# A planner that orders attention and a long convolution on one core: hand-written rules for the next task, against weighted sums with eight sets of weights

## The chip, the cores and the metric

The kernel runs on one core of a Trainium2 chip. The metric is the time of one execution in microseconds of device time. TensorE (PE) does the matmuls, VectorE (DVE) and ScalarE (ACT) empty its results from PSUM and do the elementwise work, GpSimd (POOL) issues the loads that change the type, and SyncE (SP) issues the other transfers.

## The reference

```python
# attention: batch 8, seq 3136, d_model 256, d_qk 64
scores = (1.0 / S) * np.matmul(z, z.transpose(0, 2, 1))
attn = np.maximum(scores, 0.0) ** 2
x = u * np.matmul(attn, v)
# then a gated long convolution over the sequence
proj = x @ w_proj                                  # 256 -> 768: x1, x2, x3
X2 = np.fft.rfft(x2, n=S, axis=1)
H = np.fft.rfft(filter_fft, n=S, axis=0)[None, :, :]
x2_conv = np.fft.irfft(X2 * H, n=S, axis=1)
y = x1 * x2_conv * x3
out = (y @ w_out).astype(np.float32)
```

The scores are symmetric in the two positions, and there is no softmax. The inputs are float32; the kernel computes with bfloat16 operands and float32 sums.

## The kernel before, in words

For each of the 8 batches the 3136 rows are cut into 7 chunks of columns (512, 512, 512, 512, 512, 256, 320), and for each chunk the score tiles of 128 rows are made in pairs. A score task (kind S) multiplies two 64-row operands at once in two halves of the array, or, cut further, in four quarters. ScalarE takes the relu of the pair (tile R_t, L1762), and VectorE (L1771) or ScalarE (L1769) squares it (A_t). A weighing task (kind W) multiplies the square by v and adds it up in one of two PSUM accumulators, ps_o. Some squares are also transposed by a DMA (M_t, M2e_t, M2o_t) and weighed again in a later chunk, because the scores are symmetric. At the end of a chunk VectorE multiplies the accumulators by u (xT_t, L1813), which frees them for the next chunk.

The rest of the network is made of other tasks of PE. Kind FA is a chunk's projections (wp) with the first step of its transform; their results go to gates (L1157) or through DRAM to the next step of the transform. Kind Q is the middle of the transform in quarters of the array, forward (S) and inverse (TZ), with a multiplication by the filter on VectorE (L1245) between. Kind FB ends the transform and applies w_out, and yT_t (L1331) is the gated product before that. Kind FZ holds such tasks of the last two batches that are kept back for the end. PSUM has three pairs of banks (ps_s) for all results but the weighing's; a score or a Q task takes a whole pair, the others one bank. Every matmul passes line 518, every copy out of PSUM line 551 (ScalarE) or 555 (VectorE).

No queue or loop fixes the order of this work. All tasks are first written down with what they depend on, what buffers they take and a cost in microseconds for each engine that can do them; then `Plan.go` plays the program through, always starting the task that can start first, and emits the instructions of each engine in that order. On the chip each engine goes through its own list and waits at semaphores. So the planner's choices are the order, and nothing is chosen at run time.

For PE, `pick_pe` looks at the first few tasks of each kind and goes through rules with fixed limits: stay with the scores while a pair of banks is free, go back to them when two or three pairs are free, put a Q task into a run of scores (the whole run is then cut into quarters, `plan.quarters`), do weighing or projections first by a `credit` that weighing earns (PACE) and other work spends. For the other engines, `pick` takes the task that can start first, in steps of 0.03 us, and among equals the one with the lower `prio`.

The diff touches the constants at the head of the file, these functions, and the two places that cut scores and short weighings into quarters:

Of the kernel before, what the change touches and what calls it, by code (L numbers as in the profile page):

```python
# [11 lines left out]
P = 128  # L12
# [6 lines left out]
N1 = 64  # L19
# [1 line left out]
NJ = 16  # L21
CHUNKS = (512, 512, 512, 512, 512, 256, 320)
INF = float("inf")
PACE = 0.45
HOLD = 3
DELAY = 4
GROUP = 1
BACKLOG, AMPLE, STAY = 1.5, 5.0, 0.1
LATE_PUT, LATE_LOAD, LATE_TURN, LATE_C, LATE_D2 = 3.0, 1.0, 1.5, 2.5, 1.0
SPEC_LAG = 1  # L30
LATE_F = 6.0
# [2 lines left out]
FINAL = (0, 2, 4, 6, 1, 3, 5)  # L34
ZP, ZL = 0, 0.0
MOST = 3
FULL = 3.0
QUAD, FIRST, LEAD = -INF, 1.0, 0
YIELD = 1.0
REACH = 2  # L40
SHARE = {0: 1, 2: 3}

# [117 lines left out]
class Task:  # L160


    def __init__(self, emit, cost, deps=(), takes=(), prio=0, lat=None, moves=0.0, late=0.0):
        self.emit, self.cost, self.takes, self.prio = emit, cost, list(takes), prio
        self.lat, self.moves, self.late = lat, moves, late
        self.deps = [d if isinstance(d, tuple) else (d, None) for d in deps]
        self.kids, self.frees = [], []
        self.left = len(self.deps)
        self.ready = 0.0
        self.end = None  # L170
        self.holders = 1
        for d, _ in self.deps:
            d.kids.append(self)
# [9 lines left out]
class Plan:  # L183


    def __init__(self):
        self.free = {e: 0.0 for e in ("PE", "ACT", "DVE", "SP", "POOL")}
        self.queues = {"S": [], "Q": [], "W": [], "FA": [], "FB": [], "FZ": []}
        self.pend = {e: [] for e in ("ACT", "DVE", "SP", "POOL")}
        self.credit = 0.0  # L190
        self.mode = None
        self.quarters = False
        self.quad_run = self.score_run = 0
        self.soon = False
        self.n = 0
        self.spare = []
        self.pairs = None
        self.bus = 0.0
# [70 lines left out]
    def queued(self, t):  # L269
        some = {id(x): x for e in ("ACT", "DVE") for x in self.pend[e] if x.ready <= t + 0.3}  # L270
        return sum(max(0.0, self.free[e] - t) for e in ("ACT", "DVE")) + sum(min(x.cost.values()) for x in some.values())

    def pick_pe(self):
        t = self.free["PE"]
        got = {}
        for k, window in (("S", 1), ("Q", 4), ("W", 1), ("FA", 6), ("FB", 6), ("FZ", 6)):
            best = None
            for task in self.queues[k][:window]:
# [3 lines left out]
            if best:  # L282
                got[k] = best
        if not got:
            return None
        more = self.queues["S"]
        quad = got.pop("Q", None)
        if self.mode == "S" and self.quarters and quad and quad[0] <= t + STAY:
            if not more or self.quad_run < 1 and self.score_run >= LEAD:
                return (*quad, "Q")  # L290
        if more and not more[0].left:
            left = self.backlog()
            if self.mode == "S":
                if "S" in got and got["S"][0] <= t + STAY:
                    return (*got["S"], "S")
                got.pop("S", None)
                if self.quarters and quad and quad[0] <= t + STAY and self.quad_run < 1:
                    return (*quad, "Q")
            else:
                want = 3 if left > AMPLE else 2  # L300
                free = self.pairs.when(min(want, len(more)) - 1)
                first = quad and quad[0] <= t + 0.3 and left > FIRST and self.credit > QUAD
                if "S" in got and free > t + 0.04:
                    rest = {k: v for k, v in got.items() if k != "S" and (k == "W" or left > BACKLOG)}
                    if rest and min(v[0] for v in rest.values()) < free:
                        got = rest
                    elif free < INF:
                        if first and not LEAD:
                            return max(quad[0], free), quad[1], "Q"
                        self.soon = bool(first)  # L310
                        return max(got["S"][0], free), got["S"][1], "S"
                elif "S" in got:
                    if first and not LEAD:
                        return (*quad, "Q")
                    self.soon = bool(first)
        elif quad:
            got["Q"] = quad
        if not got and quad:
            return (*quad, "Q")
        if not got:  # L320
            return None
        near = t + 0.04
        order = ["S", "Q"]
        order += ["FA", "FB", "W", "FZ"] if self.credit > 0 and self.queued(t) < FULL else ["W", "FA", "FB", "FZ"]
        for k in order:
            if k in got and got[k][0] <= near:
                return (*got[k], k)
        k = min(got, key=lambda k: (got[k][0], order.index(k)))
        return (*got[k], k)

    def pick(self, e):
        t = self.free[e]
        best = None
        for task in self.pend[e]:
            s = max(t, self.ready_at(task))
            if s == INF:
                continue
            first = next(iter(task.cost))
            if e != first:
                behind = sum(  # L340
                    x.cost[first] for x in self.pend[first]
                    if x is not task and x.prio <= task.prio and next(iter(x.cost)) == first and x.ready <= s + 0.3
                )
                end = s + task.cost[e]
                held = max((end - max(x.ready, s) for x in self.pend[e] if len(x.cost) == 1 and x.ready < end), default=0.0)
                if end + YIELD * held >= max(self.free[first], task.ready) + behind + task.cost[first]:
                    continue
            key = (round(s / 0.03), task.prio, task.no)
            if best is None or key < best[0]:
                best = (key, s, task)  # L350
        return best and (best[1], best[2], e)

    def go(self):
        while True:
            got = []
            x = self.pick_pe()
            if x:
                got.append((x[0], 0, x[1], "PE", x[2]))
            for i, e in enumerate(self.pend):
                x = self.pick(e)  # L360
                if x:
                    got.append((x[0], i + 1, x[1], e, None))
            if not got:
                break
            start, _, task, e, k = min(got, key=lambda g: g[:2])
            if k:
                self.queues[k].remove(task)
                half = k in ("S", "Q")
                if half != (self.mode == "S") and self.mode:
                    start += 0.096  # L370
                    self.quarters, self.quad_run, self.score_run = half and self.soon, 0, 0
                self.score_run += k == "S"
                if k == "Q":
                    self.quad_run += 1
                    if self.score_run and not self.quarters:
                        start += 0.092
                    self.quarters = True
                self.mode = "S" if half else k
                if k == "W":
                    self.credit = min(self.credit + PACE, 2.0)  # L380
                elif k != "S":
                    self.credit = max(self.credit - task.cost["PE"], -2.0)
            self.run(task, e, start)
        left = sum(len(q) for q in self.queues.values()) + sum(len(q) for q in self.pend.values())
        assert not left, f"{left} tasks left over"
# [3 lines left out]
def kernel(  # L389
# [12 lines left out]
    B, S, D = u.shape  # L402
# [23 lines left out]
    plan = Plan()  # L426
# [1141 lines left out]
    def score_mm(un, where):  # L1568
# [6 lines left out]
        for i in order[: len(pair)] if len(pair) != 3 else (0, 2, 1):  # L1575
            (t, at), h = pair[i], ds((i if len(pair) <= 2 else i // 2) * dqk, dqk)
            o = blocks(ps, len(pair), cw)[:, i]
            for m in range(0, P, N1 if plan.quarters else P):
                n = N1 if plan.quarters else P
                matmul(o[ds(m, n)], zt[h, ds(t * P + m, n)], zt[h, ds(C0[at], cw)], start=True, stop=True)  # L1580
        live[un] = ps

# [131 lines left out]
    def weigh_short(b, c):  # L1714
        cw = CHUNKS[c]
        un, i = short[b, c][1:]
        for dh in range(2):
            h = ds(dh * N1, N1)
            for m in range(0, P, N1 if plan.quarters else P):
                n = N1 if plan.quarters else P  # L1720
# [5 lines left out]
    for gi, g in enumerate(groups):  # L1726
# [23 lines left out]
        for i, un in enumerate(g):  # L1750
# [13 lines left out]
            def sq(e, un=un, rows=rows, n=n, cw=cw, box=box, a_p=a_p):  # L1764
# [142 lines left out]
```

## Time and profile before

| | |
|---|---|
| time, median of 3 runs | 1000.24 us (999.77 to 1001.09) |
| span of the profiled execution | 996.6 us |
| PE busy | 956.2 us, 6831 matmuls |
| ScalarE busy | 878.6 us |
| VectorE busy | 826.4 us |
| first matmul and last matmul | 4.9 us after the start, 8.0 us before the end |
| DMA moved | 170.33 MB, mean 171 GB/s |
| granted TensorE clock | 0.996 |

The span is the time from the first to the last instruction of one profiled execution, and the time of a run is some microseconds more. PE's busy time is what its matmuls cover, overlaps counted once; the ends of matmuls are modelled. The page gives such sums, groups of instructions by line, and the chain that ended last; the trace behind it gives the same for any stretch of time, what an engine waited for, and a timeline in which equal instructions in a row are merged (start, length, engine, line, count).

### The profile page before, as it was taken

How to read it: one execution, taken by the hardware profiler on the slowest of the kernel's cores; microseconds unless marked ns; L12 is line 12 of the kernel's file. 1: busy time of each engine (PE TensorE's matmuls, PEld its weight loads, DVE VectorE, ACT ScalarE, POOL GpSimd, SP SyncE). 2: the span in 40 equal slices, each digit the busy share in tenths (PEclk: the TensorE clock that was granted, in tenths of full speed). 3: DMA queues.
4: the chain of work that ended last, by engine and by line, in shares of the span. 5: the costliest groups of instructions: out<-in, count | busy, mean ns of one | idle time of the engine just before them, and what ended most of it. 6: DMA issues, size and time to landing. Idle time of an engine off the chain costs nothing. (4 is left out here: it accounts for less than half of the span.)

```text
span 996.6 us, 19588 instructions
## 1 busy us (share of the span) xinstructions
PE 956.2 (96%) x6831; PEld 470.0 (47%) x6831; DVE 826.4 (83%) x1447; ACT 878.6 (88%) x1205; POOL 187.2 (19%) x403
## 2 busy tenths in 40 slices
PE   6999999999999999999999999999999999999975
PEld 2343544346444554435544464444644356444643
DVE  8975689987788788888789878887888969889785
ACT  5987799989899898989998989999889989999774
POOL 5142311122011210213021131113201122000000
PEclk9999999999999999999999999999999999999999
DMA  9899868788998798888999888997899879865676
GB/s 157 145 176 184 142 127 176 148 158 176 196 174 149 157 177 194 177 174 140 193 204 184 150 174 167 201 187 146 160 208 182 159 137 197 210 142 126 161 217 205
DMA packets 332376, 170.33 MB, mean 171 GB/s; under 512 B 242442, under 2 KB 307786, under 8 KB 332276
## 3 DMA queue, kind: packets, MB, share of 16 engines
q1 hardware_dynamic: 304548, 138.10, 62.8%
q0 software_dynamic: 27728, 30.97, 22.3%
q8 instruction: 54, 0.88, 0.4%
q14 instruction: 46, 0.38, 0.1%
HBM read 90.26 MB, written 53.35 MB: 144 GB/s over the span
## 5 line engine op out<-in xcount | busy, mean ns | idle before, releaser
L1762 ACT ACTIVATE R_t<-ps_s 128x1024 f32<-128x1024 f32 (+4 forms) x512 | 470.3, 956 | 40.5 <-PE ps_s L518 26.2
L518 PE MATMUL ps_o_t<-A_t,v_t 128*128 128x512 bf16 (+6 forms) x2074 | 462.0, 354 | 6.3 <-DVE A_t L1771 6.0
L1771 DVE TENSOR_TENSOR A_t<-R_t 128x1024 bf16<-128x1024 f32 (+1 forms) x291 | 330.9, 1150 | 67.2 <-ACT R_t L1762 62.4
L518 PEld LDWEIGHTS <-v_t 128*128 128x128 bf16 (+1 forms) x2878 | 250.2, 98 | 271.6 <-issue 83.0
L1769 ACT ACTIVATE A_t<-R_t 128x1024 bf16<-128x1024 f32 (+4 forms) x205 | 196.4, 964 | 5.3 <-DMA M_t<-A_t 2.2
L518 PE MATMUL ps_s<-zT_t 64*64 64x512 bf16 (+4 forms) x1485 | 158.4, 359 | 2.8 <-ACT x_t L551 1.0
L601 POOL COPY tick<-xT_t 1x1 bf16<-1x1 bf16 x54 | 12.4, 230 | 709.8 <-DVE xT_t L1813 693.8
L518 PE MATMUL ps_s<-xT_t,wp 128*128 128x512 bf16 (+2 forms) x430 | 103.5, 352 | 3.8 <-DVE xT_t L1813 1.4
L551 ACT ACTIVATE x_t<-ps_s 128x512 bf16<-128x512 f32 (+2 forms) x137 | 74.1, 568 | 21.2 <-PE ps_s L518 12.7
L1813 DVE SCALAR_TENSOR_TENSOR xT_t<-ps_o_t,uT_t 128x256 bf16<-128x256 f32 (+2 forms) x224 | 76.0, 381 | 19.3 <-PE ps_o_t L518 11.5
L1245 DVE TENSOR_TENSOR xh<-xh,H 128x1024 bf16<-128x1024 bf16 x120 | 82.3, 686 | 6.6 <-ACT xh L551 2.7
L518 PEld LDWEIGHTS <-zT_t 64*64 64x64 bf16 (+1 forms) x1518 | 56.2, 101 | 66.0 <-issue 49.6
L518 PE MATMUL ps_o_t<-M_t,v_t 128*128 128x512 bf16 (+2 forms) x352 | 82.2, 353 | 0.0
L1157 DVE TENSOR_TENSOR gate_t<-ps_s,x_t 128x256 bf16<-128x256 f32 (+2 forms) x216 | 71.8, 382 | 10.5 <-PE ps_s L518 7.6
L518 PEld LDWEIGHTS <-wp 128*128 128x128 bf16 x448 | 42.7, 98 | 48.9 <-issue 11.7
L1331 DVE TENSOR_TENSOR yT_t<-ps_s,gate_t 128x512 bf16<-128x512 f32 (+2 forms) x97 | 57.8, 620 | 8.1 <-PE ps_s L518 6.4
L592 POOL DMA_DIRECT2D un_t<-in_u_dram x112 | 59.9, 555 | 7.8 <-issue 4.6
L611 POOL DMA_DIRECT2D v_t<-in_v_dram x112 | 59.5, 556 | 4.9 <-issue 2.8
L518 PE MATMUL ps_s<-wp,xT_t 128*128 128x256 bf16 x398 | 56.1, 273 | 0.3 <-DVE xT_t L1813 0.2
L551 ACT ACTIVATE gs_t<-ps_s 128x512 bf16<-128x512 f32 (+1 forms) x89 | 50.6, 605 | 5.9 <-PE ps_s L518 5.5
L518 PE MATMUL ps_s<-wo,yT_t 128*128 128x256 bf16 (+1 forms) x362 | 53.8, 273 | 1.7 <-DVE yT_t L1331 1.7
L555 DVE CAST x_t<-ps_s 128x512 bf16<-128x512 f32 (+2 forms) x73 | 46.0, 641 | 10.5 <-PE ps_s L518 8.3
(147 smaller groups left out, 824.1 us busy)
## 6 DMA issues: line engine op xcount, KB each, us to landing
out_dram<-ost_t SPq DMA_DIRECT2D x66, 256.0 KB
spec<-s_t SPq DMA_DIRECT2D x96, 128.0 KB
spec_in_t<-spec SPq DMA_DIRECT2D x60, 192.0 KB
spec<-gs_t SPq DMA_DIRECT2D x60, 192.0 KB
v_t<-in_v_dram POOLq DMA_DIRECT2D x80, 128.0 KB, 4.5
un_t<-in_u_dram POOLq DMA_DIRECT2D x80, 128.0 KB, 5.0
conv_in_t<-spec SPq DMA_DIRECT2D x33, 256.0 KB
out_dram<-ost_t SPq DMA_DIRECT2D x19, 128.0 KB
```

Of the source, the lines that this page charges most:

```text
L518: wrote(nc.tensor.matmul(o, *args, **kw), o)
L551: got = nc.scalar.activation(out_, in_, AF.Copy)
L555: got = nc.vector.tensor_copy(out_, in_)
L592: nc.gpsimd.dma_start(out=t[ds(j * N1, N1), lo - t0 : hi - t0, :], in_=x[:, n2 : n2 + hi - lo, :])
L611: nc.gpsimd.dma_start(out=t[ds(j * N1, N1), ds(v_at(a), (b - a) * D)], in_=r[:, n2 + a - lo : n2 + b - lo, :].rearrange("p t d -> p (t d)"),)
L1157: got = nc.vector.tensor_tensor(g[:, ::-1] if h == 0 else g, p, x, ALU.mult)
L1245: nc.vector.tensor_tensor(x[:, 1 - i], x[:, 0], h, ALU.mult)
L1331: got = nc.vector.tensor_tensor(yb["y"][:, dh, 0:w], p, gates[b, c, dh][:, 0:w], ALU.mult)
L1762: has_read(nc.scalar.activation(blocks(box["R"], n, cw)[:rows], p, AF.Relu), p)
L1769: nc.scalar.activation(a, r, AF.Square)
L1771: nc.vector.tensor_tensor(a, r, r, ALU.mult)
L1813: nc.vector.scalar_tensor_tensor(x, f, inv_s2, ut, ALU.mult, ALU.mult)
```

## The change

The rules in `pick_pe` go. For the first few tasks of each kind the kind's candidate is found as before, and then one number is worked out for it: how long PE would stand until it can start, plus a price for changing the array's arrangement times a weight (`turn`), plus nine weights of its kind times nine numbers of the state. These are 1, the evictions queued (`queued`), the weighing that is ready (`backlog`), the credit, the free banks, the length of the present run, the free pairs, and how long the second and the third pair still need. The lowest number is taken. Scores in a run that began in halves stay in halves; they are cut into quarters only if the run has had a Q task (`mode` 2).

The weights come from one of eight sets, "a" to "h". A string of 187 letters, MIX, names the set for each stretch of twelve PE tasks; the plan has 2244 of them. The pace at which weighing earns credit comes from the set too.

For the other engines, `pick` adds a bias by rank to the start (-0.03 to 0.09 us) in place of the steps of 0.03 us and the strict `prio`; `give` takes the place of the constant YIELD. Ranks come from `prio` by (2, 3, 4, 5, 0)[prio], so tasks with prio 4 have the same rank as those with prio -1.

```diff
-PACE = 0.45
-BACKLOG, AMPLE, STAY = 1.5, 5.0, 0.1
-FULL = 3.0
-QUAD, FIRST, LEAD = -INF, 1.0, 0
-YIELD = 1.0
+SWITCH, QUARTER = 0.096, 0.092
+KINDS = {"S": 1, "Q": 4, "W": 1, "FA": 6, "FB": 6, "FZ": 6}
+WEIGHTS = {
+    "a": Weights(
+        1.395, 0.797, 2.224, (-0.03, 0.0, 0.0, 0.03, 0.06, 0.09),
+        S=(-0.016, -0.197, 0.206, -0.053, -0.117, -0.017, -0.366, 0.385, 0.73),
+        Q=(-1.226, 0.38, -0.129, 1.049, -0.235, 0.074, -0.055, 0.599, -0.351),
+        W=(0.422, -0.009, -0.077, -0.062, 0.08, 0.007, 0.665, -0.522, 0.017),
+        FA=(-0.26, 0.123, 0.021, -0.232, 0.123, 0.099, 0.3, -0.453, -0.001),
+        FB=(0.819, -0.04, 0.086, -0.343, -0.295, 0.133, 0.206, -0.228, 0.033),
+        FZ=(2.581, -0.139, 0.697, 0.542, -0.157, 0.139, -0.368, 0.005, 0.316),
+    ),
...
+STRETCH = 12
+MIX = (
+    "chbeegbghbaageecebgfecfgbadeeedffbcgebdcgbececaahhfbceddhcdegbdhdhegdefcehbcagec"
...
+        self.rank = (2, 3, 4, 5, 0)[prio]
...
+    def weights(self):
+        return WEIGHTS[MIX[min(self.done // STRETCH, len(MIX) - 1)]]
+
+    def state(self, t):
+        at = self.pairs.banks.at
+        some, left = self.queued(t), self.backlog()
+        empty = sum(x <= t for pair in at for x in pair)
+        whole = sorted(max(pair) for pair in at)
+        second, third = ((min(max(x - t, 0.0), 2.0) if not self.mode else 0.0) for x in whole[1:])
+        return 1.0, some, left, self.credit, empty, self.length, sum(x <= t for x in whole), second, third
...
+            s, task = best
+            mode = max(self.mode or 0, 1) if kind == "S" else 2 * (kind == "Q")
+            turn = 0.0
+            if self.mode is not None and mode != self.mode:
+                turn = QUARTER if self.mode == 1 and mode == 2 else SWITCH
+            worth = s - t + turn * weights.turn
+            for w, x in zip(weights.kinds[kind], state):
+                worth += w * x
+            if got is None or worth < got[0]:
+                got = worth, s + turn, task, kind, mode
+        return got and got[1:]
...
-                if end + YIELD * held >= max(self.free[first], task.ready) + behind + task.cost[first]:
+                if end + give * held >= max(self.free[first], task.ready) + behind + task.cost[first]:
...
-            key = (round(s / 0.03), task.prio, task.no)
+            key = (s + ranks[task.rank], task.no)
...
-            for m in range(0, P, N1 if plan.quarters else P):
-                n = N1 if plan.quarters else P
+            for m in range(0, P, N1 if plan.mode == 2 else P):
+                n = N1 if plan.mode == 2 else P
...
+            r_.rank = 1
```

The last line gives the relus rank 1. No task, cost, buffer or dependence is changed.

More of the change, by code (lines that the diff above doesn't have):

```diff
@@ L40 @@
+STRETCH = 12
+MIX = (
+    "chbeegbghbaageecebgfecfgbadeeedffbcgebdcgbececaahhfbceddhcdegbdhdhegdefcehbcagec"
+    "abbbdgfdgbdhchhdchcaedhfhhaeacbaadeebfaaabfccdgdffdfaacccfebchccdabdfbdbeeccafae"
+    "fhchhgabfghcchhgdfgdeggaaaa"
+)
 REACH = 2
@@ L191, in __init__ @@
         self.mode = None
-        self.quarters = False
-        self.quad_run = self.score_run = 0
-        self.soon = False
+        self.length = self.done = 0
         self.n = 0
@@ L271, in queued @@
         return sum(max(0.0, self.free[e] - t) for e in ("ACT", "DVE")) + sum(min(x.cost.values()) for x in some.values())
+    def weights(self):
[7 more added lines that the diff above has]
+        return 1.0, some, left, self.credit, empty, self.length, sum(x <= t for x in whole), second, third
     def pick_pe(self):
-        t = self.free["PE"]
-        got = {}
-        for k, window in (("S", 1), ("Q", 4), ("W", 1), ("FA", 6), ("FB", 6), ("FZ", 6)):
+        t, weights = self.free["PE"], self.weights()
+        state = self.state(t)
+        got = None
+        for kind, window in KINDS.items():
             best = None
-            for task in self.queues[k][:window]:
+            for task in self.queues[kind][:window]:
                 s = max(t, self.ready_at(task))
@@ L281, in pick_pe @@
                     best = (s, task)
[L282 to L329, printed above, removed]
+            if best is None:
+                continue
@@ L331, in pick @@
+        return got and got[1:]
     def pick(self, e):
         t = self.free[e]
+        ranks, give = self.weights().ranks, self.weights().give
         best = None
@@ L357, in go @@
             if x:
-                got.append((x[0], 0, x[1], "PE", x[2]))
+                got.append((x[0], 0, x[1], "PE", *x[2:]))
             for i, e in enumerate(self.pend):
@@ L361, in go @@
                 if x:
-                    got.append((x[0], i + 1, x[1], e, None))
+                    got.append((x[0], i + 1, x[1], e, None, None))
             if not got:
                 break
-            start, _, task, e, k = min(got, key=lambda g: g[:2])
+            start, _, task, e, k, mode = min(got, key=lambda g: g[:2])
             if k:
                 self.queues[k].remove(task)
[L368 to L378, printed above, removed]
+                if mode != self.mode and (self.mode, mode) != (1, 2):
+                    self.length = 0
+                self.mode = mode
+                self.length += 1
                 if k == "W":
-                    self.credit = min(self.credit + PACE, 2.0)
+                    self.credit = min(self.credit + self.weights().pace, 2.0)
                 elif k != "S":
                     self.credit = max(self.credit - task.cost["PE"], -2.0)
+                self.done += 1
             self.run(task, e, start)
@@ L1718, in weigh_short @@
             h = ds(dh * N1, N1)
-            for m in range(0, P, N1 if plan.quarters else P):
-                n = N1 if plan.quarters else P
+            for m in range(0, P, N1 if plan.mode == 2 else P):
+                n = N1 if plan.mode == 2 else P
                 matmul(
```

67 lines of the change are left out of this document (added).

## The prediction

> **What bounds the kernel now.** I read the page's header and busy line first, then the busy time by stretch, then what TensorE (PE) waited for in the middle, and last the timeline around changes of its arrangement and near the end.
>
> ```profile
> span 996.6 us, 19588 instructions
> PE 956.2 (96%) x6831; PEld 470.0 (47%) x6831; DVE 826.4 (83%) x1447; ACT 878.6 (88%) x1205; POOL 187.2 (19%) x403
> 0.00:50.00 50.00, 39.38 (x206) 15.75 (x207) 44.47 (x98) 36.98 (x45) 15.99 (x40) 1.00 0.90 150
> 50.00:930.00 880.00, 865.99 (x6129) 421.36 (x6128) 737.21 (x1257) 801.60 (x1085) 171.26 (x363) 1.00 0.86 169
> 930.00:997.00 67.00, 50.80 (x500) 32.89 (x498) 44.70 (x93) 40.04 (x76) 0.00 (x0) 0.94 0.72 206
> ```
>
> The last three rows are stretches: us, then busy PE, PEld, DVE, ACT, POOL, clock, DMA share, GB/s. PE is idle 10.6 us at the start, 14.0 us in 880 us of middle, 16.2 us at the end, 40.8 in all; ScalarE and VectorE have 78 and 143 us to spare in the middle. So PE's instruction stream is the bound, and the change rewrites only its order. The profiled execution's span is 996.6 us against a median of 1000.24 us; I take the 3.6 us around the span as fixed.
>
> What ended PE's idle time in the middle (us, times, longest):
>
> ```profile
> PE ps_o_t L518 <- DVE A_t L1771: 4.0, 8, 0.8
> PE ps_o_t L518 <- DVE xT_t L1813: 3.7, 7, 1.0
> PE ps_s L518 <- ACT R_t L1762: 1.9, 3, 1.3
> PE ps_s L518 <- DVE xT_t L1813: 1.7, 5, 0.7
> PE ps_s L518 <- ACT x_t L551: 1.1, 3, 0.4
> PE ps_s L518 <- ACT s_t L551: 0.8, 2, 0.7
> PE ps_s L518 <- DVE x_t L555: 0.3, 2, 0.2
> ```
>
> Three kinds: weighing waits for a square (4.0); a chunk's turn, where VectorE must empty the accumulators, as xT_t, before the next chunk's weighing (3.7) or its own projections (1.7) can start; and a score bank that is not yet emptied (R_t, x_t, s_t, x_t: 4.1).
>
> **The change, part by part.** It alters no task. In the two instruction orders as built, DMA, POOL and full-array matmul counts are equal; 271 matmuls go (6831 to 6560), since fewer scores are cut into quarters: four 64x64 quarters and two 64x128 halves stream for the same time, so this alone is worth nothing. Rival one, that the change does not do what it says, is out: hardly a line of PE's order stays in place.
>
> *Changes of arrangement.*
>
> ```profile
> 410.28 1.04 PE L518 MATMUL ps_o_t<-A_t,v_t 128*128 128x512 bf16 x4
> 411.25 0.41 PE L518 MATMUL ps_s<-xh,TZ 64*64 64x512 bf16 x4
> 411.49 0.60 PE L518 MATMUL ps_s<-zT_t 64*64 64x512 bf16 x8
> 412.02 1.04 PE L518 MATMUL ps_o_t<-A_t,v_t 128*128 128x512 bf16 x4
> 932.85 0.43 PE L518 MATMUL ps_o_t<-A_t,v_t 128*128 128x320 bf16 x2
> 933.67 0.71 PE L518 MATMUL ps_o_t<-A_t,v_t 128*128 128x320 bf16 x4
> 934.31 0.31 PE L518 MATMUL ps_s<-zT_t 64*128 64x320 bf16 x2
> 934.45 0.30 PE L518 MATMUL ps_o_t<-A_t,v_t 64*128 64x320 bf16 x2
> 934.59 0.30 PE L518 MATMUL ps_s<-zT_t 64*128 64x320 bf16 x2
> 934.82 0.39 PE L518 MATMUL ps_s<-x_t,T 128*128 128x512 bf16 x1
> ```
>
> A 512-column matmul takes (1.04-0.39)/3 = 0.217 us from start to start, a 320-column one (0.71-0.43)/2 = 0.14. Four from 410.28 are through at 411.15 and the quarters start at 411.25; their three groups of 0.21 would be through by 411.89 and the full array starts at 412.02: a visit to quarters costs 0.23. Four from 933.67 are through at 934.23, the halves start at 934.31; the last pair is through at 934.73, the full array starts at 934.82: with rounding, 0.2 a visit. The order as built has 160 visits to halves instead of 127 and 97 to quarters instead of 123: 33 x 0.2 - 26 x 0.23 = **+0.6 us**, all on PE's path. The Trainium skill, "TensorEngine Tiling (Array Packing)", Key Properties, says that changing the tiling mode drains the array, which speaks against the 7 visits more. The trace agrees, in the 0.1 us at each edge; by that rule alone the time would be 1000.8.
>
> *Waits in the middle.* For each task of PE I counted the PE work (columns at the paces above) that the order puts between the matmul that feeds it and the task itself.
>
> Weighing after its square: the chain is relu, square, hand-overs:
>
> ```profile
> L1762 ACT ACTIVATE R_t<-ps_s 128x1024 f32<-128x1024 f32 (+4 forms) x512 | 470.3, 956 | 40.5 <-PE ps_s L518 26.2
> L1771 DVE TENSOR_TENSOR A_t<-R_t 128x1024 bf16<-128x1024 f32 (+1 forms) x291 | 330.9, 1150 | 67.2 <-ACT R_t L1762 62.4
> ```
>
> That is 2.1 us with nothing queued, and up to one more relu and square, 4.2, where the engines are busy. Tasks with under 4.5 us of cover: 57 before, 16 after. In that proportion 4.0 becomes 1.1: **-2.9** (bounds -4.0 and 0).
>
> Projections after the chunk's xT_t: under 2 us of cover 80 before, 1 after; the 1.7 goes: **-1.7**. Next chunk's weighing after it: turns with under 1.2 us of cover 10 before, 6 after; 3.7 becomes 2.2: **-1.5** (bounds -3.7 and +1).
>
> Banks: this gets worse. Reuses of a score bank with under 1.2 us of PE work since its last matmul: 56 before, 101 after (under 1.4 us: 162 and 254). What fills the room won above is projections, and their banks are turned round at once. In proportion 4.1 becomes 7.4, +3.3; but few of the 56 waited at all (10 waits on banks in the whole list), which would make it +0.9 for 45 more at 0.02. I take **+2.0**, between them.
>
> ScalarE and VectorE: about 20 squares go to VectorE and 18 copies to ScalarE. At 1.15 us the squares are 23 us more on VectorE before the copies are taken off, of its 143 spare: nothing. If that cover were gone, it would be on the path in full.
>
> Middle: -2.9 - 1.7 - 1.5 + 2.0 = **-4.1**.
>
> *The end.* The last batch's spectrum is a chain through DRAM, and what work of PE is left beside it counts.
>
> ```profile
> 942.35 0.98 PE L518 MATMUL ps_o_t<-A_t,v_t 128*128 128x320 bf16 x6
> 945.54 0.49 PE L518 MATMUL ps_s<-x_t,T 128*128 128x512 bf16 x2
> 948.91 2.92 SPq L991 DMA_DIRECT2D spec_in_t<-spec  x6
> 954.69 0.63 PE L518 MATMUL ps_s<-spec_in_t,S 49*64 49x256 bf16 x9
> 957.00:963.00 6.00, 4.18 (x68) 2.46 (x68) 6.00 (x11) 6.00 (x13) 0.00 (x0) 1.00 0.85 284
> 963.00:970.00 7.00, 5.09 (x85) 2.81 (x85) 5.92 (x11) 5.49 (x12) 0.00 (x0) 0.84 0.78 220
> 970.00:978.00 8.00, 6.94 (x36) 3.44 (x35) 4.90 (x15) 4.49 (x9) 0.00 (x0) 0.92 0.53 155
> 956.25 5.49 SPq L1390 DMA_DIRECT2D out_dram<-v_t  x6
> 971.01 1.75 SPq L1290 DMA_DIRECT2D spec<-uT_t  x3
> 973.95 4.33 SPq L1003 DMA_DIRECT2D A_t<-spec  x7
> ```
>
> The last weighing is the row at 942.35. The new order puts 10 projections of 512 columns and one transform more behind it: 11 x 0.217 = 2.4 us less stands ahead of it, and behind it PE idles 16 us anyway. The order also brings the first forward transform nearer to the last weighing (49 matmuls between, not 84) and spreads the withheld output work over 957 to 978, where PE is idle. In 957 to 970 VectorE is busy 11.92 of 13 us, so that stretch will not shrink; I count the 2.4 once: **-2.4**. Bounds: -6.5, half of what PE idles here before its last matmul on top; and +2.6 for the queue: four of the six out_dram<-v_t stores now stand in SP's queue between the spec<-uT_t puts and the last loads A_t<-spec, at 5.49/6 = 0.92 us each 3.7, of which the gap from 972.76 to 973.95 hides 1.2.
>
> The clock dips to 0.84 and 0.92 here. The Trainium skill, "TensorE: Matmul & The Clock Gate", Part 1, has the clock fall after an idle window of about 3.4 us and return after a busy one; the trace agrees in so far as the dip lies where PE idles most. By that rule a denser stretch would win at most 0.16 x 7 + 0.08 x 8 = 1.8 us more. I leave it out, since the evictions bind there.
>
> *The start.* The first 11 us of work are almost the same sequence; PE waits for data: 0 (-1 to +1).
>
> Sum: +0.6 - 4.1 - 2.4 = -5.9 on 1000.24: **994.3 us**.
>
> **Rivals.** *More is won.* If no bank waits more, the turns' 3.7 goes too and the end yields its 6.5: 0.6 - 4.0 - 1.7 - 3.7 - 6.5 = -15.3, **985**. For it: the cover grew at every data dependence. Against: bank cover shrank.
>
> *The end gives it back.* The stores ahead of the last loads delay the final chain by 2.6 and the 2.4 is lost: 0.6 - 4.1 + 2.6 = -0.9, **999.3**, no change. For it: SP's new order. Against: 164 matmuls, not 132, now follow the last inverse transform and can run beside those loads.
>
> *Slower: the banks.* A copy that finds a relu of 0.956 us on ScalarE holds its bank that much longer. The 92 more reuses under 1.4 us would, at 0.15 us each, cost 13.8 where I put 2.0: -5.9 + 11.8 = +5.9, **1006**. It turns the sign past 0.086 us each. For it: ScalarE is busy 91% of the middle. Against: reuses this close hardly waited before.
>
> **Chances.** Forecast 0.52, more 0.20, given back 0.14, banks 0.14. About 0.2% (2 us) is what a measurement of this kernel can tell from no change. Faster: 0.50 of the forecast's 0.52 and the 0.20, 0.70; same: 0.14 and the rest of the forecast's, 0.16; slower 0.14. The range leaves out most of the bank case and the far end of the big gain: 986.5 to 1001.5; the forecast's own is 990 to 998.
>
> **What would show it.** Right: middle idle of PE near 10 us with A_t and xT_t rows small and R_t and x_t rows larger; the last weighing about 6 us earlier and its distance to the end the same. Wrong: bank rows over 10 us in the middle; or PE's last matmul over 8 us before the end, with A_t<-spec issued over 4 us after the spec<-uT_t puts.

## The result, and the profile after

The changed kernel took 985.5 us, the median of four executions (981.70, 983.38, 987.62, 987.84), against 1000.38 us for the kernel before (four, 999.77 to 1001.09): a ratio of 0.9852, 95% interval 0.9825 to 0.9878. In a later round six more executions gave 988.48 us (984.62 to 991.65); over all ten the median is 987.0. Beside these six the kernel before took 1000.52 us. So the gain is 12 to 15 us where 5.9 had been forecast, and the kernel after spreads over 10 us (981.70 to 991.65) where the one before spreads over 4 (998.27 to 1002.35 in all rounds). The median of all ten lies at the edge of the forecast's range of 986.5 to 1001.5; the size of the gain was forecast at under half either way.

The profile of the 981.70 us execution of the kernel after, header and busy line:

```profile
span 979.9 us, 18879 instructions
PE 940.6 (96%) x6450; PEld 468.4 (48%) x6560; DVE 827.4 (84%) x1449; ACT 872.4 (89%) x1203; POOL 186.2 (19%) x403
```

Its busy time by stretch (us, then busy PE, PEld, DVE, ACT, POOL, clock, DMA share, GB/s), cut where its middle ends:

```profile
0.00:50.00 50.00, 39.48 (x205) 15.78 (x209) 43.01 (x96) 37.71 (x47) 16.53 (x42) 1.00 0.87 148
50.00:923.00 873.00, 861.79 (x5850) 427.44 (x5951) 746.55 (x1275) 801.44 (x1094) 169.67 (x362) 1.00 0.91 173
923.00:980.00 57.00, 39.38 (x399) 25.15 (x400) 37.89 (x79) 33.29 (x65) 0.00 (x0) 0.90 0.70 204
```

What ended TensorE's idle time in 50 to 923 us (us, times, longest):

```profile
PE ps_o_t L575 <- issue: 3.5, 22, 0.2
PE ps_s L575 <- DVE s_t L612: 2.0, 1, 2.0
PE ps_s L575 <- DMA spec_in_t<-spec: 0.9, 1, 0.9
PE ps_s L575 <- issue: 0.2, 1, 0.2
PE ps_o_t L575 <- DVE x_t L612: 0.2, 1, 0.2
```

The rows of `issue` are places where a matmul's record is missing from the trace (6450 of 6560 are there); no engine waits in them. Without them 3.1 us are left, of 13.5 before: the rows of A_t, of xT_t and of R_t have gone, and that of the copies x_t is 0.2. What stands there instead are two single waits, 2.0 and 0.9 us, that hang on transfers to and from DRAM (below). The window's idle time, 873.00 - 861.79 = 11.2 us, says less than it seems: 7.5 of it stand at 98 places of missing records, and 3.7 are idle, of 14.0 before.

Yet PE is 96% busy in both kernels, and while the middle's list fell by 10.4 us, the last weighing came 20 us earlier (943.02 to 923.02, counted at its last matmul). The reason is how a wait is drawn. Two rows of PE's timeline in the kernel before:

```profile
771.69 0.59 PE L518 MATMUL ps_o_t<-A_t,v_t 128*128 128x512 bf16 x2
773.10 1.24 PE L518 MATMUL ps_o_t<-A_t,v_t 128*128 128x512 bf16 x5 [0.81 <-DVE A_t L1771]
```

Two matmuls of 0.217 us from start to start begin at 771.69; the next could start at 772.12 and starts at 773.10, 0.97 us late after rounding. The view calls 0.81 of that idle, since it draws each matmul about 0.16 us past the start of the next. So every wait is listed 0.16 us short, and those under 0.16 us not at all. The Trainium skill, "Perfetto Trace Analysis", opening note, calls matmul busy time a bad metric for how close a kernel is to the roofline, because matmuls are pipelined; this case agrees, with 96% on both sides of a change of 15 us.

I therefore measured each kernel from start to start: the time between two matmuls less the pace of the first one's shape (0.217 us for 512 columns, shared by the matmuls that run side by side in halves or quarters) and less 0.1 us for each edge of an arrangement. The sum of the paces and edges is "work"; the rest is waiting. "Middle" runs from 35 us of work to the last weighing, "end" from there to the last matmul:

| us | before | after |
|---|---|---|
| first matmul starts | 4.9 | 5.3 |
| work | 927.7 | 928.5 |
| waits up to 35 us of work | 9.6 | 9.0 |
| waits in the middle | 30.1 | 12.6 |
| of these ahead of weighings | 18.6 | 4.9 |
| waits at the end | 16.2 | 15.6 |
| last matmul's start to the end of the span | 8.3 | 9.0 |

The middle's -17.4 is the whole gain between these two profiles; the other rows sum to +0.7, and the span falls by 16.7. Single waits over 0.4 us in the middle: some 21 with 15 us before, and after only the two named above, with 3.1 us. The sizes hang on the pace: most pairs of 512 columns start 0.2155 us apart, and with that in place of 0.217 the middle has 35.5 us before and 17.8 after. The difference stays. How the waits after fall to weighings and to the rest is uncertain by some 2 us, since 110 records are missing there.

### The profile page after: what moved, and what is told of

Its sections match the earlier page's. It is cut to its first block, busy times and chain, and to the rows that moved or that the text cites. A ratio compares the mean times of both kernels' runs of the same rounds, so it can differ in the third digit from the quotient of the medians.

```text
span 979.9 us, 18879 instructions
## 1 busy us (share of the span) xinstructions
PE 940.6 (96%) x6450; PEld 468.4 (48%) x6560; DVE 827.4 (84%) x1449; ACT 872.4 (89%) x1203; POOL 186.2 (19%) x403
## 4 chain that ended last, share of the span: by engine, by line
PE 88%; DMA 4%; DVE 3%; ACT 2%; issue 1%; SPq 1%; ACTq 0%; DVEq 0%
PE ps_o_t L575 52%; PE ps_s L575 36%; DVE A_t L1828 1%; DMA spec_in_t<-spec 1%; DMA ost_t<-in_z_dram 1%; ACT R_t L1819 1%; DMA spec<-gs_t 1%; SPq L700 1%; DMA conv_in_t<-spec 1%; DMA spec<-s_t 0%; DMA A_t<-spec 0%; DVE yT_t L1388 0%; ACT xh L608 0%; ACT gs_t L608 0%; SPq L1447 0%
## 5 line engine op out<-in xcount | busy, mean ns | idle before, releaser
L1819 ACT ACTIVATE R_t<-ps_s 128x1024 f32<-128x1024 f32 (+4 forms) x512 | 473.7, 957 | 53.6 <-PE ps_s L575 39.3
L575 PE MATMUL ps_o_t<-A_t,v_t 128*128 128x512 bf16 (+3 forms) x1998 | 465.0, 354 | 8.0 <-issue 3.5
L1828 DVE TENSOR_TENSOR A_t<-R_t 128x1024 bf16<-128x1024 f32 (+3 forms) x312 | 346.1, 1128 | 77.6 <-ACT R_t L1819 76.9
L575 PEld LDWEIGHTS <-v_t 128*128 128x128 bf16 (+2 forms) x2846 | 249.8, 98 | 271.1 <-issue 88.4
L1826 ACT ACTIVATE A_t<-R_t 128x1024 bf16<-128x1024 f32 (+4 forms) x184 | 181.2, 990 | 2.1
L575 PE MATMUL ps_s<-zT_t 64*128 64x512 bf16 (+4 forms) x1246 | 152.5, 355 | 3.3 <-DVE s_t L612 2.0
L658 POOL COPY tick<-xT_t 1x1 bf16<-1x1 bf16 x54 | 11.7, 216 | 684.7 <-DVE xT_t L1871 669.4
L608 ACT ACTIVATE x_t<-ps_s 128x512 bf16<-128x512 f32 (+2 forms) x143 | 78.6, 565 | 10.7 <-PE ps_s L575 8.0
L575 PEld LDWEIGHTS <-zT_t 64*128 64x128 bf16 (+1 forms) x1279 | 49.9, 98 | 77.7 <-issue 60.1
L608 ACT ACTIVATE xh<-ps_s 128x512 bf16<-128x512 f32 (+1 forms) x86 | 48.3, 607 | 8.8 <-PE ps_s L575 8.5
L608 ACT ACTIVATE s_t<-ps_s 128x512 bf16<-128x512 f32 x80 | 47.0, 592 | 2.3 <-PE ps_s L575 1.8
```

The source lines that it names most:

```text
L575: wrote(nc.tensor.matmul(o, *args, **kw), o)
L608: got = nc.scalar.activation(out_, in_, AF.Copy)
L658: nc.gpsimd.tensor_copy(tick[:], xt["t"][0:1, 1, 0:1])
L1819: has_read(nc.scalar.activation(blocks(box["R"], n, cw)[:rows], p, AF.Relu), p)
L1826: nc.scalar.activation(a, r, AF.Square)
L1828: nc.vector.tensor_tensor(a, r, r, ALU.mult)
```

## The experiments

Two theories were set against each other first. **P, the policy:** weighing many conditions at once picks better tasks than the old rules. **F, the fit:** the eight sets and the 187 letters spell one particular order, found by trial; the rules are only the alphabet. Four kernels took the change apart. `MIX` is the string of letters, one per twelve TensorE tasks.

### TensorE's choice alone

In the kernel after, the other engines choose as before:

```diff
-                if end + give * held >= max(...
+                if end + held >= max(...
-            key = (s + ranks[task.rank], task.no)
+            key = (round(s / 0.03), task.prio, task.no)
```

> The changed kernel with its weighted choice for TensorE, and the old choice for the other engines (steps of 0.03 us, then prio; YIELD 1.0). Theory P (policy): the weighted sums choose better whatever stands around them, and the choice for the other engines is a detail: 984 to 990 us. Theory F (fit): the weights and the 187 letters spell out one particular sequence that happens to wait little; anything that shifts the sequence early loses the whole gain: 997 to 1012 us, with over 25 us of start-to-start waits in the middle, where the changed kernel has 12.6.

Measured: 1016.87 us, ratio to before 1.0162 (1.0142 to 1.0182): 27 us past P's range, and on F's side, above its range by some 5. The waits in the middle are 35.0 us (table below).

### The other engines' choice alone

The kernel before, with the new key for ScalarE, VectorE and the queues, in set a:

```diff
+        self.rank = (2, 3, 4, 5, 0)[prio]
...
-                if end + YIELD * held >= max(...
+                if end + 0.797 * held >= max(...
-            key = (round(s / 0.03), task.prio, task.no)
+            key = (s + (-0.03, 0.0, 0.0, 0.03, 0.06, 0.09)[task.rank], task.no)
...
+            r_.rank = 1
```

> The kernel before with the changed choice for the other engines alone (ranks and give of set a), TensorE's rules as before. Theory P: the two choices add up, and this one is worth the smaller part: 996 to 1001 us. Theory F: the rules of before were themselves fitted to their own sequence, so this is slower than before: 1003 to 1018 us.

Measured: 1017.17 us, ratio 1.0171 (1.0150 to 1.0192), as F has it. Each half of the change, alone, is 16 us slower than before; together they are 15 faster. The gain does not lie in either half.

### One set for all

```diff
-MIX = ("chbeegbghbaageec..." ...)
+MIX = "a" * 187
```

> The changed kernel with set a in all 187 stretches. Theory P: the eight sets differ in a few digits, one of them does nearly as well: 984 to 990 us. Theory F: 994 to 1008 us.

Measured: 1010.01 us, ratio 1.0099 (1.0076 to 1.0122), 2 us above what F gave and 20 above P.

### The letters backwards

```diff
-MIX = ("chbeegbghbaageec..." ...)
+MIX = "aaaaggedgfdghhcc..."
```

> The changed kernel with the 187 letters in reverse, so every set is used as often as before, at another place. Theory P: 984 to 991 us, as the mix of sets is the same. Theory F: 995 to 1010 us.

Measured: 1013.51 us, ratio 1.0135 (1.0112 to 1.0158). That is 3.5 us above F's range. The same letters, each used as often, lose 26 to 28 us by their order alone.

These four speak against P as it was put: the sums, given set a alone, make a kernel 9 us slower than the old rules. F predicts something stranger, that one letter is as good as all.

### One letter of 187

```diff
-MIX = ("chbeegbghbaageec..." ...)
+MIX = ("chbeegbfhbaageec..." ...)
```

> The kernel after with one of its 187 letters changed: the eighth, g to f; the other 186 letters, all eight sets and all rules stay. P (the weighted sums choose better as such): within the spread of the kernel after, 980 to 990 us. F (the letters spell one particular order, found by trial, and each letter fits only what the ones ahead of it lead to): from the eighth stretch on the letters meet another state than the one that they were found in, so they are worth no more than one set alone. One set for all lost 1010.0 - 985.5 = 24.5 us over 187 stretches; 180 of them are left here, 24.5 x 180/187 = 23.6, so 1009 us, in a range of 1000 to 1018.

Measured: 1004.70 us (1004.42 to 1006.57), ratio 1.0057 (1.0041 to 1.0073). One letter at stretch 8 costs 18 to 19 us, more than the whole gain, and the 179 letters behind it, each unchanged, are then 5 us better than 179 times `a`. How the letters were found is not on record. That the letters behind a place fit only the order ahead of it is shown by this run and the next, for two places.

### One letter half way

```diff
-    "abbbdgfdgbdhchhdchca..."
+    "abbbdgfdgbddchhdchca..."
```

> The kernel after with one other letter changed, the 92nd of 187 (h to d), half way through. P: 980 to 990 us. F: the first half stays as it was and keeps its gain; 95 stretches are left to the wrong letters, 24.5 x 95/187 = 12.4 us, so 998 us, in a range of 992 to 1005, and the trace shows the waits of TensorE up to about half of its work as in the kernel after and those behind it as with one set alone.

Measured: 1009.61 us (ten executions, 1000.18 to 1011.99), ratio 1.0076 (1.0047 to 1.0104). The median misses F's range by 5 us, the place is as expected. From start to start, waits per 100 us of work:

| us of work | 300 | 400 | 500 | 600 | 700 | 800 |
|---|---|---|---|---|---|---|
| after | 0.7 | 0.7 | 0.5 | 1.1 | 1.0 | 1.3 |
| letter 92 changed | 0.7 | 1.2 | 2.9 | 4.1 | 2.8 | 5.6 |
| one set | 3.7 | 1.9 | 1.4 | 2.9 | 1.1 | 3.2 |

Up to the letter, half way through the tasks, the kernel keeps the gain; behind it the waits are worse than with one set, so my estimate in proportion to the letters left was wrong. Another part of the miss has nothing to do with letters: the two DRAM waits named above, ahead of the letter and in the same order, took 5.9 and 3.9 us in this profile, not 2.2 and 1.0 (from start to start). The ten executions, 12 us apart, fit such waits.

Where the time of these kernels went, against the kernel after (visits as built):

| kernel | visits to halves, quarters | work | waits in the middle | waits at the end | span |
|---|---|---|---|---|---|
| before | 127, 123 | 927.7 | 30.1 | 16.2 | 996.6 |
| after | 160, 97 | 928.5 | 12.6 | 15.6 | 979.9 |
| TensorE's choice alone | 200, 106 | 938.7 | 35.0 | 18.4 | 1015.3 |
| the others' choice alone | 131, 122 | 928.2 | 45.5 | 18.3 | 1015.7 |
| one set | 195, 109 | 938.1 | 28.0 | 18.6 | 1007.2 |
| letters backwards | 194, 109 | 937.8 | 33.2 | 17.4 | 1010.7 |
| letter 8 changed | 195, 111 | 938.4 | 23.8 | 18.1 | 1002.4 |
| letter 92 changed | 181, 106 | 934.6 | 34.1 | 19.0 | 1009.0 |

Where the new choice of TensorE runs off its letters from early on, it makes 34 to 40 visits to halves more than the kernel after, and its work is 9 to 10 us more. Work counts 0.1 us for each edge by its definition, so its rise is no test of the prediction's price of a visit. The edges themselves are: in the kernel after the median edge behind matmuls of 512 columns adds 0.097 us to their pace on the way into halves and out of them, 0.093 into quarters and 0.103 out. So a visit costs 0.19 to 0.20 us; the prediction's 0.2 holds, and its 0.23 is 0.03 high.

### What the order hides: a faster square

F says where the gain comes from, not what the order does. Theory W: it puts more work between a square and the weighing that needs it. Then a square that is done sooner should help the kernel before much and the kernel after little. In both kernels, with no instruction moved:

```diff
-                box["R"] = R_p.tile()
+                box["R"] = R_p.tile([P, 2, 512], BF16)
```

> The kernel before with its tile R_t (relu of the scores, ahead of the square) in bfloat16 instead of float32; each engine's order of instructions stays as it was. The scores are rounded once more. The square on VectorE then reads bfloat16: 1219 ns should become about 690 (the product xh<-xh,H of the same 128x1024 tile in bfloat16 took 686). 244 squares, some 129 us of VectorE, and each square's tile lands some 0.5 us earlier. Theory W (the 30 us that TensorE lost in the middle is work that stands in line ahead of its data, 18.6 of it weighings that wait for a square): the waits fall with the latency, 6 to 14 us off, 987 to 995 us. Rival L (the loss lies in the order and the pace of ScalarE, which has 479 relus and stays as it is): at most 3 us off, 997 to 1001.

> The same edit of R_t in the kernel after, order unchanged. Theory W: only 4.9 us of waits ahead of weighings are left there, so at most 4 us off, 981 to 986 us, and the two kernels come to within 2 to 8 us of each other, from 15. Rival L: 982 to 986, and the distance between the two kernels stays at 12 to 15 us.

Measured: the kernel before falls to 990.85 us (989.58 to 993.07), ratio 0.9913 (0.9890 to 0.9937); the kernel after to 983.43 (982.25 to 985.82), 0.9843 (0.9824 to 0.9862), 2 us under its first 985.5 and so within its spread. The group of the squares on VectorE without the edit and with it, and then, with it, the middle's waits of weighings and the busy line, all in the kernel before:

```profile
L1771 DVE TENSOR_TENSOR A_t<-R_t 128x1024 bf16<-128x1024 f32 x244 | 294.6, 1219 | 56.3 <-ACT R_t L1762 51.8 <-ACT A_t L1769 3.7
L1771 DVE TENSOR_TENSOR A_t<-R_t 128x1024 bf16<-128x1024 bf16 x244 | 167.2, 688 | 91.8 <-ACT R_t L1762 85.5 <-DMA M_t<-A_t 5.4
```

```profile
PE ps_o_t L518 <- DVE xT_t L1813: 1.9, 4, 0.8
PE ps_o_t L518 <- DVE A_t L1771: 0.5, 2, 0.3
```

```profile
PE 946.3 (96%) x6733; PEld 470.2 (47%) x6831; DVE 692.6 (70%) x1447; ACT 874.2 (88%) x1205; POOL 185.9 (19%) x403
```

The square took 688 ns, as its neighbour of equal shape had promised (the Trainium skill, "VectorE: DVE Perf Modes", What auto-detection actually checks, has the engine take a mode of twice the rate if every tensor is of 16 bits and read in steps of one; 1219 to 688 agrees in direction, with a ratio of 1.77). The row of A_t goes from 4.0 us to 0.5, and from start to start the waits ahead of weighings from 18.6 to between 10 and 12 (98 records are missing with the edit). The distance between the kernels shrinks from 14.9 us (13.4 by all ten executions of the kernel after) to 7.4, as theory W had it: with a shorter square in both, about half of the distance is gone. Rival L, which allowed 3 us, is out for the kernel before. One thing this edit does not separate: it also frees 134 us of VectorE, so what stands behind a square in VectorE's line comes earlier too, and the row of xT_t falls from 3.7 to 1.9. That the square's own latency is most of it is argued, not shown.

### The spread of the kernel after

Six times the same order, 7 us apart. Its slower profile (990.50 us, span 988.7) shows where. VectorE, then PE:

```profile
72.87 0.68 DVE L612 CAST x_t<-ps_s 128x512 bf16<-128x512 f32 x1
78.22 0.69 DVE L612 CAST s_t<-ps_s 128x512 bf16<-128x512 f32 x1 [4.66 <-issue]
```

```profile
279.93 1.03 PE L575 MATMUL ps_o_t<-A_t,v_t 128*128 128x512 bf16 x4
284.78 0.63 PE L575 MATMUL ps_s<-spec_in_t,S 49*64 49x256 bf16 x2 [3.82 <-DMA spec_in_t<-spec]
285.78 1.06 PE L575 MATMUL ps_s<-spec_in_t,S 49*64 49x512 bf16 x8 [0.37 <-DMA spec_in_t<-spec]
```

The copy into s_t waits for one of three tiles whose store to DRAM has not landed (in the bfloat16 twin the same gap is put down to `DMA specf<-s_t`), 3.2 us in the fast profile and 4.7 here; the load of a spectrum at 280 us is late by 0.9 there and 3.8 here. From start to start, waits between 200 and 300 us of work are 1.6 us in one and 8.2 in the other, and all of the middle 12.6 and 21.1: that is 8.4 of the 8.8 us between the spans. Between 300 and 900 us of work the two profiles have the same 6 us of waits: what spreads lies ahead of that.

Three kernels went with that run, all in the order of the kernel after.

```diff
-    s1_p = Pool("s1", 3, [P, 2, D], BF16)
+    s1_p = Pool("s1", 6, [P, 2, D], BF16)
+    s1_p.slots = Slots(3)
```

> The kernel after with six tiles behind the pool of s_t (the copy of a spectrum on its way to DRAM) instead of three; the plan is still made for three, so each engine's order of instructions stays as it was, and only the wait for a tile's last store goes. Theory B: what spreads the runs of the kernel after over 981.7 to 987.8 us is VectorE's copy into s_t at 77 us, which waits for the DMA specf<-s_t of three tiles ahead to land and holds TensorE up by 2.2 us in the profiled run of 981.7 and 5.3 us in that of the same order with bfloat16 (983 to 986). With three more tiles that wait goes: 979 to 983 us, and all runs within 3 us of each other. Rival: the landing is only waited for at the next place (the load of specf, or the load spec_in_t<-spec at 280 us), then 984 to 987 with the spread as it was.

> The kernel after as it is, beside the others on the same chip, for its spread: 980 to 989 us, median 985.

> The kernel after with R_t in bfloat16 and six tiles of s_t, order unchanged; the scores are rounded once more. If the two act on different waits their effects add: 2 us from bfloat16 (983.4 against 985.5 measured) and 2 to 5 us from the tiles, 977 to 982 us. If bfloat16 was only a luckier spread: the same as with six tiles alone.

Measured: six tiles 983.95 us (981.19 to 986.61), the kernel after 988.48 (984.62 to 991.65), both edits 980.60 (976.24 to 988.13); ratios to before 0.9836 (0.9817 to 0.9856), 0.9881 (0.9858 to 0.9904) and 0.9820 (0.9795 to 0.9846). VectorE in the kernel with six tiles:

```profile
73.11 0.69 DVE L613 CAST s_t<-ps_s 128x512 bf16<-128x512 f32 x1 [0.19 <-PE ps_s L576]
77.16 0.43 DVE L1521 COPY zd_t<-zn_t 128x1024 bf16<-128x1024 bf16 x1 [3.36 <-DMA zn_t<-in_z_dram]
```

The wait for the tile is gone, 5 us earlier the copy is done, and the next instruction in VectorE's line waits 3.36 us for a load of z instead. TensorE's wait for the spectrum, which the rival had named, is there too. Its row in 50 to 300 us, with six tiles:

```profile
PE ps_s L576 <- DMA spec_in_t<-spec: 3.6, 2, 3.2
```

So the rival's mechanism is seen, at the place it named and at one that it did not. The means of the runs differ by 4.4 us, with about 4 to either side (95%, from the spread of the runs), so theory B has at most part of the time, and not the spread (5.4 us left, where it gave 3). The kernel after itself came 3 us above the 985 that I had expected of it. With both edits the median is within its range of 977 to 982, and the mean is 7.0 us under that of the kernel after in the same round, with about 5 to either side: the lowest median here, at the price of a coarser rounding of the scores. Four to six executions of each do not part the two effects.

The last kernel bears on the end:

```diff
+                if b == B - 2 and c in (0, 1):
+                    return
```

> The kernel after without the four stores out_dram<-ost_t (256 KB each) of two chunks of the seventh batch, which stand ahead of the last stores spec<-s_t on the DMA queue of SyncE; that part of the output stays unwritten. Theory D: they delay the chain that TensorE waits for at the end (last weighing, last transform, store, load, first forward transform: 8.9 us from the last transform to the first forward one in both kernels), so the first forward transform starts 2 to 4.5 us earlier and the time falls by 2 to 4.5 us against the kernel after in these rounds. Rival: the chain is bound by the latency of its own stores and loads: at most 1 us off.

Measured: 983.79 us (977.19 to 990.46), ratio 0.9830 (0.9798 to 0.9862); against 988.48 that is within the spreads, so the time decides nothing. The traces say more. SP's queue and PE near the end, in the kernel after:

```profile
921.74 2.75 SPq L1447 DMA_DIRECT2D out_dram<-ost_t  x4
924.58 2.57 SPq L1018 DMA_DIRECT2D spec<-s_t  x3
930.42 2.85 SPq L1048 DMA_DIRECT2D spec_in_t<-spec  x6
```

```profile
922.34 0.98 PE L575 MATMUL ps_o_t<-A_t,v_t 128*128 128x320 bf16 x6
925.20 0.48 PE L575 MATMUL ps_s<-x_t,T 128*128 128x512 bf16 x2
934.32 1.39 PE L575 MATMUL ps_s<-spec_in_t,S 49*64 49x256 bf16 x11 [4.07 <-DMA spec_in_t<-spec]
```

and without the stores:

```profile
923.51 3.54 SPq L1018 DMA_DIRECT2D spec<-s_t  x3
928.02 2.81 SPq L1048 DMA_DIRECT2D spec_in_t<-spec  x6
```

```profile
932.43 1.43 PE L575 MATMUL ps_s<-spec_in_t,S 49*64 49x256 bf16 x11 [2.85 <-DMA spec_in_t<-spec]
```

From the start of the last transform to the first forward one it is 8.9 us with the stores (925.41 to 934.32, and 8.5 in the slower profile) and 7.7 without (924.73 to 932.43). In these profiles a megabyte of stores ahead goes with 0.8 to 1.2 us, and the 7.7 us stay without it. That fits the rival, which allowed 1 us, and not theory D's 2 to 4.5; but it is one profile without the stores, and landings move by more than 1 us between profiles, so the size is not shown.

## Why the prediction was wrong, point by point

The direction was right, the size was not: 994.3 us and a range from 986.5, against 985.5. The step that failed is the middle: -4.1 forecast, -17.4 between the profiles (-9.0 with the slower profile of the kernel after). It has three parts, which the points below take one by one: 7.0 us that the list of waits does not hold, the banks (-1.9 where +2.0 was taken) and the data waits (-9.4 where -6.1 was taken); a new wait of 0.9 for a load goes the other way. By its own steps, in the profiled executions:

- **Changes of arrangement, +0.6.** Work rose by 0.8, at 0.1 us an edge, which the edges themselves bear out. Right.
- **Weighing after its square, -2.9; next chunk's turn, -1.5; projections, -1.7.** The mechanism was right: the new order puts more work between a result and its use. These listed waits did not shrink in proportion to the places of little cover, they went: A_t, xT_t ahead of weighings and xT_t ahead of projections together from 9.4 to under 0.2 us. So the three are -9.4 in the list, where I took -6.1.
- **Banks, +2.0.** Wrong in sign: R_t, x_t and s_t from 4.1 to 2.2, and of those 2.0 is the one copy that waits for a store. A score bank came back with under 1.2 us of work in between 101 times instead of 56, and the list shows one wait of 0.2 us for such a copy. The row I had written down against it (reuses this close hardly waited before) was the better guide.
- **The base.** The largest part of the failed step: I summed the rows of a list, 13.5 us, as if they were all that TensorE loses in the middle. From start to start it was 30.1 before and 12.6 after. The listed part fell by 10.4 and the unlisted by 7. The sign that I had named for a right forecast, middle idle near 10 us, reads 11.2 in the window and 3.7 without the missing records: by the second it failed, as it should.
- **The end, -2.4.** It gave nothing: 2.3 us of work did move behind the last weighing (its place in the work falls from 898.45 to 896.12), but from the last weighing to the end it takes 56.9 us instead of 53.6. Of these 3.3 us 2.3 are the work that moved and 0.8 the work of the arrangements, counted above. My reason was that PE idles 16 us there anyway; it did not fill that time (waits at the end 16.2, then 15.6). From the last weighing to the first forward transform it takes 11.3 us (11.7 before) with 6.7 us of work in them (9.1), and PE waits 4.07 us at 934.32; behind that stand 25.7 us of work instead of 20.1, and they take 3.7 us longer. The work went behind the chain, not beside it. The sign of a right forecast, the last weighing 6 us earlier at the same distance from the end, reads 20 us earlier and 3.3 us farther. The sign that I had named for the rival "the end gives it back" came in both parts: the last matmul ends 8.7 us before the end, and in SP's queue of the kernel after

```profile
953.36 1.34 SPq L1347 DMA_DIRECT2D spec<-uT_t  x3
954.79 2.86 SPq L1447 DMA_DIRECT2D out_dram<-v_t  x4
957.76 4.23 SPq L1060 DMA_DIRECT2D A_t<-spec  x7
```

  the loads A_t<-spec stand 4.4 us behind the puts, with the four stores between. TensorE then waits 0.75 us for A_t at 961.44, where it waited for none of them before: the mechanism is there, at a third of the 2.6 that I had given it (2.5 by its own rows).
- **The start, 0.** First matmul +0.4, waits -0.6. Right.
- **ScalarE and VectorE, nothing.** Nothing speaks against it: VectorE is busy 827.4 us where it was 826.4, ScalarE 872.4 where it was 878.6, and the data waits fell all the same.

The rival "more is won" (985) named the time with other terms: its weighing and turn terms held, its -6.5 at the end did not come, and the unlisted 7 us filled its place. That its sum meets the time is luck.

What I did not ask is how far the weights fit this one plan. That a letter decides 19 us could not be read from the profile, and it does not change the forecast; a sum over the built order can cost such a change, if the base and the banks are right.

## What to carry to other kernels

Before you scale a list of waits, measure the bound engine from start to start: here the drawing of the matmuls hid the first 0.16 us of each wait in "busy", and the list showed under half of 30 us. A planner with hundreds of fitted numbers can be a stored order: judge it by the order as built. Here each of five edits to it (two single letters, one set, the letters reversed, half of its rules) lost the fit and landed 4 to 16 us above the time of the rules that it replaced; whether a new fit would win it back was not tried. To learn what an order hides, shorten the latency that you suspect in both kernels with no instruction moved, and see how far they come together.

## What the hardware showed

- A store to DRAM and the load behind it took 7.7 us from the transform to the next use even with none of the output's stores ahead of them in SP's queue, and 8.5 to 8.9 with four stores of 256 KB there. Landings moved between the profiles of the same order: the spectrum at 280 us came 0.9 us late in one and 3.8 in another. The kernel after spreads over 10 us where the kernel before, with 30 us of waits, spreads over 4; that an order with little slack passes such delays on fits this and is not shown by itself.
- Behind the 4.07 us of waiting at 934.32 the clock is down. The stretch behind it, in the kernel after, and below it the same eleven matmuls in the kernel before, which came without a wait:

```profile
934.30:940.00 5.70, 4.76 (x58) 3.38 (x59) 4.71 (x8) 3.74 (x8) 0.00 (x0) 0.51 0.90 263
954.69 0.84 PE L518 MATMUL ps_s<-spec_in_t,S 49*64 49x256 bf16 x11
```

  The granted clock is 0.51 there, just where the last chain runs, and the eleven matmuls take 1.39 us instead of 0.84. The Trainium skill, "TensorE: Matmul & The Clock Gate", Part 1, has the clock halved after an idle window of about 3.4 us. The wait of 4.07 us fits that; two shorter ones show that less is enough here, and the measurement decides. Without the four stores the wait is 2.85 us and the clock is 0.51 from 932.4 to 938 us all the same, with 1.43 us for the eleven. In the kernel before the clock is 0.50 from 967.81 to 971.20 us, right behind a wait of 1.05 us, and in the 3.4 us ahead of that TensorE was busy 1.89. No run here fills the gap to see what it is worth.
